# A fused attention and gated MLP block on one core: a regrouped prologue, other engine lists, and full-array gate matmuls for the second to last chunk

## The chip, the cores and the metric

The kernel runs on one core of a Trainium2 chip. Its engines work side by side, each on its own list of instructions in the order written: PE (TensorE, matmuls, with PEld for its weight loads), ACT (ScalarE), DVE (VectorE), POOL (GpSimd) and SP (SyncE, which here only issues DMA transfers). They wait for each other through semaphores. The metric is the device time of one launch in microseconds, as the median of several runs. The kernel before takes 939.43 us (three runs, 938.72 to 939.80).

## The reference

Input x has 2048 rows of 640 values in bf16. A first half is attention without a mask, with 32 heads of 20 values each; a second half is a gated MLP of width 1728.

```python
h  = x + attention(layernorm(x), wqkv, 32 heads) @ wo
g  = layernorm(h) @ w_gate
u  = layernorm(h) @ w_up
h2 = h + (gelu(g) * u) @ w_down
```

Attention is softmax(q k^T / sqrt(20)) v for each head, so 32 x 2048 x 2048 exponentials are taken, about 134 million. The layer norms have no weights.

## The kernel before, in words

**A planner writes the order.** The kernel is not written as loops that run on the chip. Every operation is entered with its engine, an estimated duration, a priority, and the data it reads and writes (class Sched, method op). A list scheduler (method schedule) then picks, for each engine, what comes next by its own model of time, and emit writes one straight list of instructions for each engine with the waits that are needed. A change of a duration, a priority or an engine can so reorder everything behind it. Between two modes of an engine the planner adds a cost of its own, MODE_SWITCH, 0.1 for PE. PE has three modes in it: "row" (the score matmuls, 32 rows of the array each), "col" (32 columns of the array each) and "full" (the whole array). Where PE would be idle for long the planner inserts matmuls on dummy data, to keep the PE clock up (function idle; they read wo or x and gk).

**Prologue.** x is loaded by SP in eight transfers of two row tiles each (a row tile is 128 rows; list XLS gives the tiles of each transfer). The q and k part of wqkv is loaded when the transfer that holds tile 4 has landed, the v part when the one with tile 11 has landed (XG), and wo after that. For each group of four tiles come the statistics of the layer norm (ln_stats on DVE, or ln_stats_act on ACT, by list LNS), 1/sqrt(variance) for the four together (ln_rsqrt: sqrt on ACT, reciprocal on DVE), the normalisation itself (ln_apply, by list LNE), five PE transposes, and the copy of their result from PSUM (list LNV). Statistics of a tile on ACT are two passes with a read of the accumulator behind each. Then proj makes k of the first four heads for all 2048 rows and q for the first 512, with priorities G0P; proj_v makes v. The first score matmul needs all of these.

**Attention.** Queries go in seven chunks, of 512, 512, 256, 256, 256, 128 and 128 rows (CHUNKS). The chunks are cut in 32 slots, and each slot in 64 score tiles of 128 x 512, 2048 tiles in all. A unit is two or three tiles: PE makes their scores (row mode) in two or three PSUM banks, ACT takes the exponential of all banks of the unit in one instruction, PE multiplies by v (col mode) into bank 6. List PATS says for each slot whether units alternate between three and two tiles ('2') or are all of three tiles ('3'). List DS says, for each slot as a hex digit, how many units give their third tile to DVE, which computes the exponential in integer and polynomial steps (d_exp), two tiles together.

**MLP and what lies behind a chunk.** When the slots of a chunk are done, function post enters its output projection, second layer norm (here ln_rsqrt has no sqrt, but a bit trick and two Newton steps on DVE), transposes, gates, ups and downs. They run as background work of PE and DVE under the attention of the next chunks. Gate results are copied by DVE (L1081) into an SBUF array, ACT applies gelu to it later in a few long instructions (each time it has to change its function table), DVE multiplies by the ups (L1100), and the downs are added to h by DVE (L1117). For chunk 5, the second to last (GT = (5,)), gelu, ups and downs are held until the last exponential, but its gates run under the attention of chunk 6. In background work a 128-column matmul is issued as four matmuls of 32 columns of the array each (quarters, line 664 of the profile). Operations carry an alternative as one full-array matmul (whole, line 660) that the planner uses only before the first and after the last score matmul.

The tail is what follows the last exponential: the rest of chunk 5, and all that chunk 6 needs.

Of the kernel before, what the change touches and what calls it, by code (L numbers as in the profile page):

```python
# [6 lines left out]
ALU = mybir.AluOpType  # L7
# [3 lines left out]
I32 = mybir.dt.int32  # L11
# [7 lines left out]
DMA_RATE = 0.36  # L19
DT = 0  # L20
LATE = (0, 1, 2, 3, 4)
LNS = [{'a': 'act', 'd': 'dve'}[x] for x in 'dddddaaaddddddaa']
LNE = [{'a': 'act', 'd': 'dve', 'p': 'pool'}[x] for x in 'dddadaddddaaadda']
LNV = [{'a': 'act', 'd': 'dve'}[x] for x in 'dadadddaadaaadad']
SLIP = 0.0
WARM = 3.4
KEEP = 0.5
# [23 lines left out]
class Sched:  # L51
# [10 lines left out]
    def op(self, eng, fns, dur, prio, reads=(), writes=(), acq=(), rel=(), after=(), sem=None, lat=None, mode=None, mb=0.0, alt=None):  # L62
        if self.evp is not None and eng == "dve" and rel and prio >= P_EPI:
            prio = self.evp
        o = Op()
        o.i = len(self.ops)
        o.eng, o.dur, o.lat, o.sem = eng, dur, LAT[eng] if lat is None else lat, sem
        o.mode = mode
        o.mb = mb
        o.alt = alt  # L70
        o.tag = writes[0] if writes else None
        o.fns = fns if isinstance(fns, list) else [fns]
        o.prio = (prio, o.i)
        deps = set(after)
        for r in reads:
            if r in self.lw:
                deps.add(self.lw[r])
        for w in writes:
            if w in self.lw:
                deps.add(self.lw[w])  # L80
            deps.update(self.rd.get(w, ()))
        for r in reads:
            self.rd.setdefault(r, []).append(o.i)
        for w in writes:
            self.lw[w] = o.i
            self.rd[w] = []
        deps.discard(o.i)
        o.deps = deps
        o.acq = list(acq)
        o.rel = list(rel)  # L90
        o.succ = []
        o.ready = 0.0
        o.start = None
        o.group = None
        self.ops.append(o)
        return o.i
# [230 lines left out]
RSQRT_MAGIC = float(0x5F3759DF)  # L327
# [12 lines left out]
VAG = 13  # L340
P1E = 'dd'
P1 = 1
XLS = (2,2,2,2,2,2,2,2)
XG = (4,11)
POOLT = 1.0
LNM = 'd'
# [6 lines left out]
XLAG = 0.85  # L353
XLG0 = 0.5
HG = 1
GT = (5,)
XPL = 1
KPR = 3.0
TFIRST = 0.0
PRE = 0.2  # L360
G0P = (2.5, 1.5, 2.5, 2.5, 1.5)
G0E = [{'a': 'act', 'd': 'dve'}[x] for x in 'dddda']


def bass_sequential_preLN__mha_block__glu_gated_geglu__prompt_kernel(
# [12 lines left out]
    with ExitStack() as es:  # L378
        sc = Sched(nc)
        op = sc.op  # L380
# [4 lines left out]
        def I(method, *args, **kwargs):  # L385
            return lambda eng: getattr(eng, method)(*args, **kwargs)  # L386


        def c_mm(n, passes=1):
            return 0.003 + passes * n / 2400.0  # L390
# [92 lines left out]
        def bank(b, n=512):  # L483
            return PS[:, 512 * b.b:512 * b.b + n]
# [45 lines left out]
        def xkey(t):  # L530
            return xof[t]

        xof, t0 = [], 0
        for i, n in enumerate(XLS):
            xof += [f"x_{i}"] * n
# [40 lines left out]
        def ln_rsqrt(t0, n, prio, need_nm=0):  # L576
            ts = range(t0, t0 + n)
            y, v = rs[:, t0:t0 + n], mv[:, t0:t0 + n, 1]
            a, b = nw[:, 0, 0:n], nw[:, 1, 0:n]
            vk, rk = [("mv", t) for t in ts], [("rs", t) for t in ts]  # L580
            d = lambda fn, r, w: op("dve", fn, 0.14, prio, reads=r, writes=w)
            if need_nm:

                op("act", I("activation", a, v, ACT.Sqrt, bias=epsc[:, 0:1]), 0.19, prio, mode="sqrt", reads=vk + ["eps"], writes=["nw0", "sd"])
                d(I("reciprocal", y, a), ["nw0"], rk)
                if need_nm == 1:
                    d(I("scalar_tensor_tensor", out=nm[:, t0:t0 + n], in0=y, scalar=-1.0, in1=mv[:, t0:t0 + n, 0],
                        op0=ALU.mult, op1=ALU.mult), rk + vk, [("nm", t) for t in ts])
                return
            d(I("tensor_scalar", a, v, LN_EPS, None, ALU.add), vk, ["nw0"])  # L590
            d(I("tensor_scalar", b.bitcast(I32), a.bitcast(I32), 1, None, ALU.logical_shift_right), ["nw0"], ["nw1"])
            d(I("tensor_scalar", y.bitcast(I32), b.bitcast(I32), -1.0, RSQRT_MAGIC, ALU.mult, ALU.add), ["nw1"], rk)
            for _ in range(2):
                d(I("tensor_tensor", b, y, y, ALU.mult), rk, ["nw1"])
                d(I("scalar_tensor_tensor", out=b, in0=b, scalar=-0.5, in1=a, op0=ALU.mult, op1=ALU.mult),
                  ["nw0", "nw1"], ["nw1"])
                d(I("scalar_tensor_tensor", out=y, in0=b, scalar=1.5, in1=y, op0=ALU.add, op1=ALU.mult),
                  ["nw1"] + rk, rk)

        def ln_apply(eng, src, dst, dkey, t, rkeys, prio):  # L600
# [32 lines left out]
        def sc_id():  # L633
            _id[0] += 1
            return _id[0]
# [4 lines left out]
        for t0 in range(0, NT, 4):  # L640
            sa = [t for t in range(t0, t0 + 4) if LNS[t] == "act"]
            for t in range(t0, t0 + 4):
                (ln_stats_act if t in sa else ln_stats)(x_sb[:, t, :], t, [xkey(t)], P_EPI)
            if sa:
                assert sa == list(range(sa[0], sa[-1] + 1))
                op("dve", I("tensor_scalar", mv[:, sa[0]:sa[-1] + 1, 1], mv[:, sa[0]:sa[-1] + 1, 1], 1.0 / D, None, ALU.mult), 0.14,
                   P_QK, reads=[("mv1", t) for t in sa], writes=[("mv", t) for t in sa])
            ln_rsqrt(t0, 4, P_QK, 1)
            for t in range(t0, t0 + 4):
                e_ops.append(ln_apply(LNE[t], x_sb[:, t, :], xn_p[:, t % 4, :], ("xnp", t % 4), t, [xkey(t)], P_QK))  # L650
                transposes(xn_p[:, t % 4, :], [("xnp", t % 4)], xnT[:, :, t * 128:(t + 1) * 128], ("xnT", t),
                           ALLB, P_EPI, LNV[t])
                e_ops.append(len(sc.ops) - 2)
# [5 lines left out]
        def whole(out, l, r, start, stop):  # L659
            return [lambda eng: eng.matmul(out()[0:l.shape[-1]], l, r, start=start, stop=stop, skip_group_check=True)]  # L660

        def quarters(out, l, r, start, stop):
            m = l.shape[-1]
            return [lambda eng, j=j: eng.matmul(out()[j:j + 32], l[:, j:j + 32], r, start=start, stop=stop,  # L664
                                                tile_position=(0, j), skip_group_check=True) for j in range(0, m, 32)]
# [97 lines left out]
            tiles += [(s_, g, kb, j) for g in gs for kb in range(NT // nk) for j in range(4)]  # L763
            slot_end.append(len(tiles))

        PATS = '22222222222322232222222332223322'
        DS = '06418768558877797888786986867867'
        PAT = [((0, 1, 2), (3, 4, 5)) if PATS[i] == '3' else ((0, 1, 2), (3, 4)) for i in range(len(slots))]
        units, ubank, upos = [], [], []
        i = 0  # L770
# [154 lines left out]
        for s_, (c, gs) in enumerate(slots):  # L925
            us = [u for u, tl in enumerate(units) if len(tl) == 3 and all(x[0] == s_ for x in tl)]
            n = int(DS[s_], 16)
            us = us[1:len(us) - DTAIL]
# [50 lines left out]
        def post(c, banks, tail):  # L979
            p = P_EPI if tail else P_BG - PRE * (c >= PREC)  # L980
            q0, nq = CHUNKS[c]
# [10 lines left out]
            for tt in range(nt):  # L992
# [10 lines left out]
                for hf in range(2):  # L1003
                    bk = Bank(*banks)
# [11 lines left out]
            if tail:  # L1016
                op("act", I("activation", nm[:, 0:1], off0[:], ACT.Gelu_apprx_tanh), 0.06, -1, mode="gelu", reads=["off0"],
                   writes=["pre"], after=(sc.lw["sd"],))
# [5 lines left out]
            p, pre = P_BG - TFIRST * tail, p  # L1024
# [11 lines left out]
            def mms(k, w, wkey, after, p=p):  # L1036
                bk, key = Bank(*banks), ("bk", sc_id())
                for fi in range(min(fn_, NF - k * fn_)):
                    f = k * fn_ + fi
                    mf = min(128, DFF - 128 * f)  # L1040
                    for a in range(NA):
                        st = fi == 0 and a == 0
                        op("pe", quarters(lambda fi=fi: bank(bk)[:, fi * nq:(fi + 1) * nq], w[:, a, f * 128:f * 128 + mf],
                                          hnT[:, a, hb * 128:hb * 128 + nq], a == 0, a == NA - 1),
                           c_mm(nq), p, mode="col", alt=whole(lambda fi=fi: bank(bk)[:, fi * nq:(fi + 1) * nq],
                                                              w[:, a, f * 128:f * 128 + mf], hnT[:, a, hb * 128:hb * 128 + nq],
                                                              a == 0, a == NA - 1), reads=hk + [wkey], writes=[key], acq=[bk] if st else [],
                           after=after if st else ())
                return bk, key
# [19 lines left out]
            else:  # L1069

                cp, gl = [], []
                for k in range(nb):
# [3 lines left out]
                    w_ = wid(k)  # L1076
                    if k >= nb - HG and c not in GT:
                        hold.append((k, bg, kg, m, fv, fk, w_))
# [3 lines left out]
                                 reads=[kg], writes=fk, rel=[bg], after=first))  # L1082
# [39 lines left out]

            if c in GT:
                def later(ba):
# [12 lines left out]
        if XPL:  # L1137
            op("act", I("activation", nm[:, 0:1], off0[:], ACT.Exp, scale=0.0), 0.06, P_QK, mode="exp", reads=["off0", ("xnT", 15), ("xnT", 14)],
               writes=["xpl", ("nm", 0)])
        for c in range(4):  # L1140
            proj("k", 0, c, PRO, G0P[c], G0E[c], True)
        proj("q", 0, 0, PRO, G0P[4], G0E[4], True)
        k3 = sc.lw["k", 0, 3]
# [16 lines left out]
        for s_, (c, gs) in enumerate(slots):  # L1160
            if c == 0:
                g = s_
# [70 lines left out]
```

## Time and profile before

| what | value |
|---|---|
| median of the runs | 939.43 us |
| the profiled execution | 939.73 us, span 937.9 us |
| ACT busy | 904.2 us, 96% of the span |
| PE busy | 877.7 us, 94% |
| DVE busy | 794.5 us, 85% |
| first exponential starts | 32.86 us |
| last exponential ends | 908.4 us |
| instructions | 33402 |
| granted TensorE clock | 1.0 over the span |

The span is the time from the first to the last instruction in the profiled execution; the 1.8 us between it and that execution's time lie outside the instructions. Nearly all lines of the program are entered through one helper, line 386, so groups are told apart by their tiles: exponentials write pts or rege from ps (PSUM), score matmuls read qt_all and kt_all, gates, ups and downs read regw (the weights). In a profile line a number behind x is a count of instructions. A time in square brackets is how long the engine sat idle before, and what ended that.

### The profile page before, as it was taken

Reading aid. Unit: us, or ns where it says so; the run is one execution under the profiler, and the core shown is the slowest. Engines: PE = TensorE matmul, PEld = TensorE weight load, DVE = VectorE, ACT = ScalarE, POOL = GpSimd, SP = SyncE. Lnnn points to the kernel's source line nnn. Section 1 sums busy time; section 2 is a strip of 40 time slices with the busy share of each in tenths; the row PEclk is TensorE's granted clock in tenths of the full one; section 3 lists DMA queues with packets and bytes.
Section 4 is the critical chain, followed back from the end, with each engine's and each line's share of the span. In section 5 each row is a group of like instructions: output and inputs, shape, how many; then the busy total and the mean of one; then the engine's idle time right before and its main releaser. Section 6 shows DMA issues by size and latency. Waiting matters only on the chain.

```text
span 937.9 us, 33402 instructions
## 1 busy us (share of the span) xinstructions
PE 877.7 (94%) x15201; PEld 386.6 (41%) x15203; DVE 794.5 (85%) x1749; ACT 904.2 (96%) x884; POOL 11.2 (1%) x45
## 2 busy tenths in 40 slices
PE   5999999999999989999999999999889999989998
PEld 3433332222233222323343333344445654556666
DVE  8659768999999999688999996988998787898673
ACT  7999999999999999999999999999999999999891
POOL 4000000000000000000000000000000000000000
PEclk9999999999999999999999999999999999999999
DMA  7010000000000160000100000011000010000000
GB/s 253 2 30 2 2 1 2 1 1 2 1 2 2 33 253 2 1 1 17 43 3 1 2 2 2 2 31 26 7 3 3 3 31 17 17 4 3 5 18 15
DMA packets 11820, 19.90 MB, mean 21 GB/s; under 512 B 608, under 2 KB 9760, under 8 KB 11680
## 3 DMA queue, kind: packets, MB, share of 16 engines
q1 hardware_dynamic: 11680, 17.78, 5.7%
q8 instruction: 119, 1.95, 0.9%
q14 instruction: 21, 0.17, 0.1%
HBM read 15.16 MB, written 2.62 MB: 19 GB/s over the span
## 4 chain that ended last, share of the span: by engine, by line
ACT 74%; PE 20%; DVE 4%; POOL 1%; issue 1%; POOLq 0%
ACT pts L386 44%; ACT rege L386 29%; PE ps L664 7%; PE ps L386 7%; PE ps L660 4%; DVE rege L386 2%; PE ps L618 1%; POOL regw L386 1%; DVE stats L386 0%; DVE qt_all L386 0%; PE ps L952 0%; DVE rege L1100 0%; DVE kt_all L694 0%; ACT L1087 0%; ACT rege L1087 0%
## 5 line engine op out<-in xcount | busy, mean ns | idle before, releaser
L386 ACT ACTIVATE pts<-ps 128x1024 bf16<-128x1024 f32 (+1 forms) x482 | 549.3, 1345 | 3.2 <-PE ps L386 3.0
L386 ACT ACTIVATE rege<-ps 128x1024 bf16<-128x1024 f32 (+1 forms) x312 | 363.6, 1328 | 1.4 <-PE ps L386 1.3
L386 PE MATMUL ps<-qt_all,kt_all 32*128 32x256 bf16 (+2 forms) x3584 | 311.2, 288 | 36.1 <-ACT pts L386 16.4
L386 PEld LDWEIGHTS ps<-qt_all,kt_all 32*128 32x128 bf16 x3584 | 96.5, 92 | 275.8 <-ACT pts L386 130.6
L664 PE MATMUL ps<-rege,regw 128*32 128x256 bf16 (+2 forms) x2970 | 158.7, 308 | 5.1 <-issue 2.3
L386 PE MATMUL ps<-pts,v_all 128*21 128x256 bf16 (+2 forms) x1956 | 157.7, 292 | 0.4 <-DVE osb L386 0.3
L386 PE MATMUL ps<-rege,v_all 128*21 128x256 bf16 (+2 forms) x1394 | 129.4, 294 | 0.0
L664 PE MATMUL ps<-regw 128*32 128x512 bf16 (+1 forms) x1656 | 120.5, 358 | 1.0 <-DVE v_all L749 0.5
L386 DVE TENSOR_TENSOR rege<-rege 128x1024 bf16<-128x1024 bf16 (+3 forms) x170 | 108.4, 641 | 1.0
L386 DVE TENSOR_SCALAR qt_all<-ps 128x512 int16<-128x512 f32 x110 | 75.3, 685 | 16.0 <-PE ps L386 15.5
L664 PEld LDWEIGHTS ps<-rege,regw 128*32 128x32 bf16 x2970 | 73.3, 96 | 37.6 <-issue 17.5
L386 DVE TENSOR_SCALAR rege<-rege 128x1024 bf16<-128x1024 int16 (+3 forms) x225 | 87.3, 398 | 1.3
L386 DVE TENSOR_TENSOR qt_all<-qt_all 128x1024 bf16<-128x1024 bf16 (+3 forms) x124 | 82.3, 664 | 1.2
L664 PE MATMUL ps<-regw,rege 128*32 128x320 bf16 x1484 | 79.3, 301 | 0.3 <-DVE rege L1100 0.3
L386 DVE TENSOR_SCALAR rege<-ps 128x512 int16<-128x512 f32 x103 | 70.5, 684 | 9.0 <-PE ps L386 8.5
L386 DVE TENSOR_SCALAR qt_all<-qt_all 128x1024 bf16<-128x1024 int16 (+3 forms) x182 | 73.3, 408 | 1.9
L386 PEld LDWEIGHTS ps<-pts,v_all 128*21 128x21 bf16 x1956 | 46.4, 90 | 60.6 <-issue 52.5
L386 PEld LDWEIGHTS ps<-rege,v_all 128*21 128x21 bf16 x1394 | 38.4, 90 | 42.1 <-issue 35.1
L386 PE MATMUL ps<-wo,gk 128*21 128x256 bf16 x296 | 52.6, 274 | 0.0
L664 PEld LDWEIGHTS ps<-regw 128*32 128x32 bf16 x1656 | 37.8, 95 | 34.8 <-issue 15.9
L1100 DVE TENSOR_TENSOR rege<-rege,ps 128x512 bf16<-128x512 bf16 (+2 forms) x53 | 35.8, 676 | 13.1 <-PE ps L664 12.8
L664 PEld LDWEIGHTS ps<-regw,rege 128*32 128x32 bf16 x1484 | 35.8, 95 | 22.2 <-issue 13.7
(109 smaller groups left out, 727.3 us busy)
## 6 DMA issues: line engine op xcount, KB each, us to landing
rege<-in_A_x_dram SPq DMA_DIRECT2D x11, 320.0 KB, 4.7
out_dram<-rege SPq DMA_DIRECT2D x16, 160.0 KB, 1.9
regw<-in_B_w_gate_dram SPq DMA_DIRECT2D x1, 2160.0 KB, 9.2
regw<-in_B_w_up_dram SPq DMA_DIRECT2D x1, 2160.0 KB, 14.1
regw<-in_B_w_down_dram SPq DMA_DIRECT2D x1, 2080.0 KB, 19.2
rege<-in_A_wqkv_dram SPq DMA_DIRECT2D x1, 1600.0 KB, 9.0
rege<-in_A_x_dram SPq DMA_DIRECT2D x2, 640.0 KB, 4.4
regw<-in_A_wqkv_dram SPq DMA_DIRECT2D x1, 800.0 KB, 8.0
```

The costliest lines, as they stand in the source:

```text
L386: return lambda eng: getattr(eng, method)(*args, **kwargs)
L618: op("pe", lambda eng, a=a: eng.transpose(bank16(bk, D)[:, 128 * a:128 * a + 128], src[:, a * 128:(a + 1) * 128], ident[:]), 0.056, prio, ...
L660: return [lambda eng: eng.matmul(out()[0:l.shape[-1]], l, r, start=start, stop=stop, skip_group_check=True)]
L664: return [lambda eng, j=j: eng.matmul(out()[j:j + 32], l[:, j:j + 32], r, start=start, stop=stop, tile_position=(0, j), skip_group_check=T ...
L1100: hdone.append(op("dve", lambda eng, bu=bu, fv=fv, m=m, w_=w_: eng.tensor_tensor(fv, fv, bank(bu, w_)[0:m, :], ALU.mult), c_dve(w_), p, re ...
```

## The change

- XLS goes from eight transfers of two tiles to five of 2, 2, 4, 4 and 4 tiles. By XG the q and k weights then wait for a transfer of tiles 4 to 7, in the place of 4 and 5; the v weights wait for tiles 8 to 11, in the place of 10 and 11.
- LNS, LNE, LNV: other tiles go to ACT. Statistics on ACT for 4 tiles in the place of 5, normalisation on ACT for 9 in the place of 6, copies on ACT for 7 in the place of 8.
- G0P: other priorities for the first projections.
- The bit trick in ln_rsqrt takes one DVE instruction less (the shift is folded into a multiplication by -0.5). The path with LNG is not used, as LNG is 0.
- PATS has seven slots with '3' in the place of six, and DS sums to 216 tiles in the place of 213; both also move between slots.
- The gates of chunk 5 are full-array matmuls (FW = 1): 70 matmuls in the place of 270, entered in mode "full".

```diff
-LNS = [{'a': 'act', 'd': 'dve'}[x] for x in 'dddddaaaddddddaa']
-LNE = [{'a': 'act', 'd': 'dve', 'p': 'pool'}[x] for x in 'dddadaddddaaadda']
-LNV = [{'a': 'act', 'd': 'dve'}[x] for x in 'dadadddaadaaadad']
+LNS = [{'a': 'act', 'd': 'dve'}[x] for x in 'dddaddaaddddddda']
+LNE = [{'a': 'act', 'd': 'dve', 'p': 'pool'}[x] for x in 'daaadaaaadadaddd']
+LNV = [{'a': 'act', 'd': 'dve'}[x] for x in 'dddaadddadaaddaa']
...
-XLS = (2,2,2,2,2,2,2,2)
+XLS = (2, 2, 4, 4, 4)
...
+LNG = 0
+LNGT = 0.2
+FW = 1
...
-G0P = (2.5, 1.5, 2.5, 2.5, 1.5)
+G0P = (2.2, 1.5, 0.5, 2.2, 0.5)
...
-            d(I("tensor_scalar", b.bitcast(I32), a.bitcast(I32), 1, None, ALU.logical_shift_right), ["nw0"], ["nw1"])
-            d(I("tensor_scalar", y.bitcast(I32), b.bitcast(I32), -1.0, RSQRT_MAGIC, ALU.mult, ALU.add), ["nw1"], rk)
+            d(I("tensor_scalar", y.bitcast(I32), a.bitcast(I32), -0.5, RSQRT_MAGIC, ALU.mult, ALU.add), ["nw0"], rk)
...
-        PATS = '22222222222322232222222332223322'
-        DS = '06418768558877797888786986867867'
+        PATS = '22222222222332232222223332223222'
+        DS = '03518768559878787888887976887868'
...
-                        op("pe", quarters(lambda fi=fi: bank(bk)[:, fi * nq:(fi + 1) * nq], w[:, a, f * 128:f * 128 + mf],
+                        wh = FW and c in GT
+                        op("pe", (whole if wh else quarters)(lambda fi=fi: bank(bk)[:, fi * nq:(fi + 1) * nq], w[:, a, f * 128:f * 128 + mf],
                                           hnT[:, a, hb * 128:hb * 128 + nq], a == 0, a == NA - 1),
-                           c_mm(nq), p, mode="col", alt=whole(lambda fi=fi: bank(bk)[:, fi * nq:(fi + 1) * nq],
+                           c_mm(nq), p, mode="full" if wh else "col", alt=None if wh else whole(lambda fi=fi: bank(bk)[:, fi * nq:(fi + 1) * nq],
```

More of the change, by code (lines that the diff above doesn't have):

```diff
@@ L590, in ln_rsqrt @@
             d(I("tensor_scalar", a, v, LN_EPS, None, ALU.add), vk, ["nw0"])
-            d(I("tensor_scalar", b.bitcast(I32), a.bitcast(I32), 1, None, ALU.logical_shift_right), ["nw0"], ["nw1"])
-            d(I("tensor_scalar", y.bitcast(I32), b.bitcast(I32), -1.0, RSQRT_MAGIC, ALU.mult, ALU.add), ["nw1"], rk)
-            for _ in range(2):
-                d(I("tensor_tensor", b, y, y, ALU.mult), rk, ["nw1"])
-                d(I("scalar_tensor_tensor", out=b, in0=b, scalar=-0.5, in1=a, op0=ALU.mult, op1=ALU.mult),
+            d(I("tensor_scalar", y.bitcast(I32), a.bitcast(I32), -0.5, RSQRT_MAGIC, ALU.mult, ALU.add), ["nw0"], rk)
+            if LNG:
+                g = lambda fn, r, w: op("pool", fn, LNGT, prio, reads=r, writes=w)
+            else:
+                g = d
+            for _ in range(2):
+                g(I("tensor_tensor", b, y, y, ALU.mult), rk, ["nw1"])
+                if LNG:
+                    g(I("tensor_tensor", b, b, a, ALU.mult), ["nw0", "nw1"], ["nw1"])
+                    g(I("tensor_scalar", b, b, -0.5, 1.5, ALU.mult, ALU.add), ["nw1"], ["nw1"])
+                    g(I("tensor_tensor", y, y, b, ALU.mult), ["nw1"] + rk, rk)
+                    continue
+                g(I("scalar_tensor_tensor", out=b, in0=b, scalar=-0.5, in1=a, op0=ALU.mult, op1=ALU.mult),
                   ["nw0", "nw1"], ["nw1"])
-                d(I("scalar_tensor_tensor", out=y, in0=b, scalar=1.5, in1=y, op0=ALU.add, op1=ALU.mult),
+                g(I("scalar_tensor_tensor", out=y, in0=b, scalar=1.5, in1=y, op0=ALU.add, op1=ALU.mult),
                   ["nw1"] + rk, rk)
```

## The prediction, made before the changed kernel was run

> **What bounds the kernel now.** I read the page first, then a table of stages, then the waits of the late stage and its timeline.
>
> ```profile
> span 937.9 us, 33402 instructions
> PE 877.7 (94%) x15201; PEld 386.6 (41%) x15203; DVE 794.5 (85%) x1749; ACT 904.2 (96%) x884; POOL 11.2 (1%) x45
> q8 instruction: 119, 1.95, 0.9%
> ```
>
> ACT is busy 96% of the span. PE with its weight loads is 30,404 of the 33,402 instructions, and they are fetched by a queue of their own: 119 packets, so about 256 instructions in each (30,404 / 119 = 255.5). The table of stages shows where each engine is full.
>
> ```profile
> core 0: us, PE busy (x) PEld busy (x) DVE busy (x) ACT busy (x) POOL busy (x), PEclk, DMA share, GB/s
> 4.00:10.00 6.00, 0.00 (x0) 0.00 (x0) 5.84 (x21) 3.08 (x8) 5.05 (x17) 1.00 1.02 347
> 16.50:26.00 9.50, 9.31 (x96) 6.42 (x99) 9.10 (x28) 9.31 (x17) 0.41 (x1) 1.00 0.32 91
> 32.90:842.00 809.10, 767.86 (x12627) 310.09 (x12630) 701.61 (x1526) 807.02 (x764) 0.00 (x0) 1.00 0.05 16
> 877.50:886.30 8.80, 6.47 (x297) 4.72 (x286) 2.75 (x6) 6.20 (x7) 0.00 (x0) 1.00 0.02 4
> 886.30:908.40 22.10, 21.77 (x669) 13.49 (x670) 20.31 (x44) 22.08 (x23) 0.00 (x0) 1.00 0.04 12
> 908.40:938.00 29.60, 25.87 (x330) 20.26 (x328) 11.33 (x25) 8.90 (x12) 0.00 (x0) 1.00 0.05 18
> ```
>
> From 32.9 to 842 us ACT is idle for 2.1 of 809 us: the exponentials set the time. In the tail (908.4 on) PE is the busiest. One stretch, 877.5 to 886.3, has all three engines idle at once: PE for 2.3 us, ACT for 2.6, DVE for 6. Its rows, from the waits of PE and the timelines of ACT and PE:
>
> ```profile
> PE ps L664 <- issue: 2.3, 3, 1.1
> ```
> ```profile
> 882.65 1.45 ACT L386 ACTIVATE pts<-ps 128x1536 bf16<-128x1536 f32 x1 [1.22 <-PE ps L386]
> ...
> 886.29 1.94 ACT L386 ACTIVATE rege<-ps 128x1024 bf16<-128x1024 f32 x2 [1.27 <-PE ps L386]
> ```
> ```profile
> 878.19 0.51 PE L664 MATMUL ps<-rege,regw 128*32 128x128 bf16 x17 [0.30 <-issue]
> ...
> 881.93 0.34 PE L664 MATMUL ps<-rege,regw 128*32 128x128 bf16 x9 [0.87 <-issue]
> ...
> 885.68 0.23 PE L664 MATMUL ps<-rege,regw 128*32 128x128 bf16 x1 [1.13 <-issue]
> ```
> ```profile
> 881.90:885.65 3.75, 2.62 (x128) 1.00 0.02 4
> ```
>
> PE stops three times, 0.30 + 0.87 + 1.13 = 2.3 us, and waits for no other engine. Each stop stands before a gate matmul of chunk 5 (128-wide, line 664), in the middle of a run of them. The restarts are 3.74 and 3.75 us apart, and between two of them there are 128 matmuls, with as many weight loads 256 instructions: one packet. So PE has eaten its stock of instructions and gets 256 in each 3.75 us, 14.6 ns for each. ACT's two waits, 1.22 + 1.27 = 2.49 us, end right behind the second and third stop, on score matmuls queued behind the gates. The Trainium skill, "Runtime: NRT & Kernel Launch", section "Instruction fetch mechanics", says that instructions come in blocks of 256 and that crossing a block is mostly hidden. The trace agrees with the 256; in this stretch it isn't hidden (0.30, 0.87, 1.13 us).
>
> **The change part by part.**
>
> *Gates of chunk 5 as full-array matmuls.* 270 matmuls become 70, and with their weight loads 400 instructions less. At 14.6 ns each that is 5.8 us less to fetch, more than the 2.3 us lacking. So I take all three stops away. Against it stand streaming and mode changes; rows from the chain of waits and from PE's timeline:
>
> ```profile
> 853.60 0.39 PE ps L618 x5
> ```
> ```profile
> 876.84 0.22 PE ps L664 x16
> ```
> ```profile
> 922.60 8.33 PE L660 MATMUL ps<-rege,regw 128*128 128x128 bf16 x140
> ```
>
> Quarters run at 0.22 / 16 = 13.8 ns while instructions last, 270 of them 3.7 us. Full ones run at 8.33 / 140 = 59.5 ns (here in the tail), 70 of them 4.2 us: +0.5 us. Five full-array transposes between two other modes cost 0.39 us where five at 59.5 would cost 0.30: 0.09 us for the change of mode. The gates lie in about 11 bursts; some half of them follow a score matmul directly, where a mode change is paid today too, the others follow v matmuls of the same mode and would pay one more: +0.5 us (0 to 1.0). In PE's account: -2.3 + 0.5 + 0.5 = -1.3 us; in ACT's: -2.5 us, if the planner puts the bursts where ACT doesn't wait. PE is nearly full from 886 us to the end, so what PE pays comes out in the tail. I take the middle, **-1.8 us**. Bounds: -2.5, and +1.5 if the stops stay (0.5 + 1.0). The Trainium skill, "TensorEngine Tiling (Array Packing)", section "Key Properties", speaks against the change: changing the tiling mode drains the array. The 0.09 us agrees with it; were it paid by every burst at both ends (22 x 0.09 = 2.0), PE's account would be +0.2 and the part worth nothing.
>
> *PATS and DS.* The price of an exponential, from the chain:
>
> ```profile
> 94.46 4.09 ACT pts L386 x4
> 98.55 2.75 ACT rege L386 x3
> ```
>
> Three of two tiles take 2.75 us, 0.917 each; four with one of three tiles 4.09, so that one 1.34. A tile costs 0.423 us, an instruction by itself 0.07. Cutting the 2048 tiles by the two lists gives 794 exponentials before and 790 after, on 1835 and 1832 tiles: 3 x 0.423 + 4 x 0.07 = 1.55 us less on ACT. ACT is never idle for long between 33 and 842 us, so this comes out nearly whole; what falls in the last two slots, where PE is full, may not. I take **-1.3 us** (0 to -1.55). DVE pays for it:
>
> ```profile
> L386 DVE TENSOR_TENSOR rege<-rege 128x1024 bf16<-128x1024 bf16 x112 | 76.4, 684 | 0.8
> L386 DVE TENSOR_SCALAR qt_all<-ps 128x512 int16<-128x512 f32 x110 | 75.3, 685 | 16.0 <-PE ps L386 15.5
> L386 DVE TENSOR_SCALAR rege<-rege 128x1024 bf16<-128x1024 int16 x112 | 46.8, 419 | 1.0
> ```
> ```profile
> 240.00:360.00 120.00, 114.70 (x251) 1.00 0.16 57
> ```
>
> Two tiles take 2 x 0.685 + 3 x 0.684 + 4 x 0.419 = 5.1 us, so three more tiles up to 7.7 us. DVE is idle for 143 us of the span, but for only 5.3 between 240 and 360 us, where slot 10 gets one tile more and where nothing stands between DVE being full and ACT waiting for banks. I cost it at nothing, with that cover; a rival below takes it away.
>
> *The shorter bit trick.* One DVE instruction of a chain of eight less, for six chunks, all under attention (this is chunk 5's, on the path neither before nor after; ACT's exponentials hide it):
>
> ```profile
> 868.64 0.15 DVE L386 TENSOR_SCALAR nw<-nw 128x1 int32<-128x1 int32 x1
> ```
>
> 6 x 0.15 = 0.9 us of DVE, taken as 0.
>
> *Prologue.* SP's issues, ACT's first work, the wait for the weights, and the prices:
>
> ```profile
> 0.75 4.49 SPq L386 DMA_DIRECT2D rege<-in_A_x_dram  x8
> 6.47 0.37 SPq L386 DMA_DIRECT2D rege<-in_A_wqkv_dram  x1
> ```
> ```profile
> 6.47 0.74 ACT L386 ACTIVATE xn_t<-rege 128x640 bf16<-128x640 bf16 x1 [4.24 <-DMA rege<-in_A_x_dram]
> ```
> ```profile
> POOL regw L386 <- DMA rege<-in_A_wqkv_dram: 2.7, 1, 2.7
> ```
> ```profile
> L386 DVE BATCH_NORM_STATS2 stats<-rege 128x6 f32<-128x320 bf16 x22 | 9.5, 465 | 0.4 <-DMA rege<-in_A_x_dram 0.3
> L386 DVE TENSOR_SCALAR rege<-rege,mv,rs 128x640 bf16<-128x640 bf16 x10 | 4.1, 458 | 0.0
> L628 DVE COPY regw<-ps 128x640 bf16<-128x640 bf16 x8 | 3.8, 478 | 0.3 <-PE ps L618 0.2
> ```
> ```profile
> L386 ACT ACTIVATE rege<-rege,nm,rs 128x640 bf16<-128x640 bf16 x6 | 5.3, 915 | 0.2 <-DVE nm L386 0.2
> L625 ACT ACTIVATE regw<-ps 128x640 bf16<-128x640 bf16 x8 | 5.3, 702 | 0.2 <-PE ps L618 0.2
> L386 ACT ACTIVATE xn_t<-rege,mv 128x640 bf16<-128x640 bf16 x5 | 4.1, 815 | 0.0
> ```
>
> Work: ACT does 3 normalisations more (+2.7 us), one set of statistics less (two passes, -1.6) and one copy less (-0.7): +0.4. DVE does statistics of one tile more (+0.9), 3 normalisations less (-1.4), one copy more (+0.5): 0. Start: ACT sits idle for 4.24 us, until tile 5 lands at 6.47. Now its first tile is number 3, of the second transfer. That has the same size as before and two transfers, each some 0.9 us (0.33 MB at the 347 GB/s of the row from 4 to 10 us), less ahead of it than tile 5's, so ACT starts some 1.6 us earlier, and the rsqrt of the first four tiles no longer queues behind a long tile on ACT. Earlier start less added work, shared by two engines that are both full from 16.5 to 26 us: (1.6 - 0.4) / 2 = 0.6; with fewer DMA issues on SP (4.49 / 8 = 0.56 us each, three less, not on the path but in favour) I take **-0.7 us**. Against it: the q and k weights are issued when the four-tile transfer lands, which is two tiles or about 0.9 us later than 6.47. They stand behind the rest of x in the queues anyway, so most of this is hidden; if not, POOL's pad waits 0.9 us longer and all projections behind it. Order by G0P can gain or lose as much again. Bounds: -2.0 and +2.0.
>
> **Sum.** -1.8 - 1.3 - 0.7 = -3.8 us. The profiled execution took 939.73 us, 1.8 more than its span and 0.3 more than the median; taken from the median, 939.43 - 3.8 = **935.6 us**.
>
> **The rivals.**
>
> 1. *The gates give nothing.* The stops go, but mode changes and slower streaming spend it on a PE that is full to the end, or the stops come from something else. For it: PE 98% busy from 886 us. Against: the 128 matmuls between stops, and 0.09 us for a mode change. Late part 0: 939.4 - 2.0 = 937.4 us, and up to 938.9 at the bound of +1.5.
> 2. *The prologue gets longer.* The weights come 0.9 us later, and the PE, full from 16.5 us on, passes it all on; with a bad order +1.2 in the place of -0.7: 937.5 us.
> 3. *DVE becomes the bound, and the kernel slower.* The place is slots 8 to 13 (DVE idle 4%) and the last slot, which gets one tile more. If all 7.7 us fell where DVE is full, ACT would wait for it and its own saving be worth nothing: -1.8 - 0.7 + 7.7 = +5.2 us. It decides (over 0.2% slower) from 4.4 us, some 57% of the added work. At two thirds: 939.4 + 2.6 = 942.0 us. For it: the 95% between 240 and 360. Against: only one of the net additions lies there, and DVE idles 143 us in all.
>
> **How the numbers follow.** A measurement can tell about 0.2%, 1.9 us: faster is below 937.55, slower above 941.3. Forecast 0.62 (its own range 933.4 to 937.2, from -2.5 - 1.55 - 2.0 to the sum without the prologue's and half of the gates' gain); rival 1 0.14; rival 2 0.10; rival 3 0.14. Faster: 0.60 of the forecast, 0.05 of rival 2, 0.01 of rival 1 = 0.66. Slower: 0.13 of rival 3 and 0.01 of rival 2 = 0.14. Same: the remaining 0.20. The range goes from 932.9 (the sum of the best bounds, 933.4, and half a microsecond of scatter) to 940.2, which takes in rivals 1 and 2 and leaves out most of rival 3.
>
> **What would show it.** Right: no wait of PE on issue and no wait of ACT on PE over 1 us between 870 and 890; gates as 128*128 at about 60 ns; 790 exponentials; the first one some 0.7 us before 32.86, the last some 3 to 4 us before 908.4; a tail of about 29.5 us as now. Wrong: PE stops at other places, more L660 downs between the last exponential and the last layer norm (a longer tail), ACT waits in slots 8 to 13 while DVE is full, or the pad on POOL starting a microsecond later than now with the first exponential behind 33.

## The result, and the profile after

The changed kernel takes 935.92 us (median of 9 runs, 935.14 to 937.89), the kernel before 939.51 us over 9 runs. The ratio is 0.9963, with a 95% interval of 0.9955 to 0.9971: faster by 0.37%. Forecast were 935.6 us, in a range of 932.9 to 940.2.

The page of the changed kernel begins so; below it are its fetch queue and the table of stages (columns as before):

```profile
span 933.9 us, 32919 instructions
PE 877.2 (94%) x14957; PEld 385.5 (41%) x14959; DVE 797.4 (85%) x1762; ACT 902.6 (97%) x878; POOL 10.7 (1%) x45
q8 instruction: 117, 1.92, 0.8%
```
```profile
877.50:886.30 8.80, 8.80 (x231) 6.43 (x225) 5.71 (x12) 8.80 (x10) 0.00 (x0) 1.00 0.02 5
886.30:905.00 18.70, 18.34 (x513) 11.00 (x510) 17.38 (x36) 18.67 (x19) 0.00 (x0) 1.00 0.04 12
905.00:938.00 33.00, 25.90 (x306) 20.19 (x303) 11.05 (x24) 6.89 (x11) 0.00 (x0) 0.98 0.05 16
```

Between 877.5 and 886.3 PE and ACT were busy 6.47 and 6.20 of 8.80 us, and now both all the time (the last stretch of the table reaches 4 us past the end of the span). No wait of PE on issue is left between the first and the last exponential, and the gates are full-array matmuls that start some 57 ns apart (in the row below 1.07 us, less the 0.22 of one matmul, over 15):

```profile
877.58 1.07 PE L671 MATMUL ps<-rege,regw 128*128 128x128 bf16 x16
```

The fetch queue moved two packets less, and PE has 244 matmuls and as many weight loads less on record.

The span falls in three parts if it is cut at the first exponential and at the function table load behind the last one. Rows of ACT's timeline, before and then after:

```profile
32.86 3.71 ACT L386 ACTIVATE pts<-ps 128x1536 bf16<-128x1536 f32 x3
...
908.39 1.28 ACT L386 ACT_TABLE_LOAD   x1
```
```profile
33.38 3.71 ACT L389 ACTIVATE pts<-ps 128x1536 bf16<-128x1536 f32 x3
...
902.97 1.28 ACT L389 ACT_TABLE_LOAD   x1
```

| part | before, us | after, us | difference | forecast |
|---|---|---|---|---|
| prologue, to the first exponential | 32.86 | 33.38 | +0.5 | -0.7 |
| attention | 875.5 | 869.6 | -5.9 | -3.1, counting the middle value for the gates |
| tail, to the end of the span | 29.5 | 30.9 | +1.4 | 0 |
| span | 937.9 | 933.9 | -4.0 | -3.8 |

So the sum came out right and its parts did not. ACT's waits on PE in the attention part, before and then after:

```profile
ACT pts L386 <- PE ps L386: 3.0, 3, 1.6
ACT rege L386 <- PE ps L386: 1.3, 1, 1.3
```
```profile
ACT rege L389 <- PE ps L389: 0.4, 1, 0.4
```

4.3 us of waits became 0.4. The page counts 485 + 305 = 790 exponentials where there were 794; at the prices of the prediction that is 1.55 us less. 3.9 + 1.55 = 5.45 us of the 5.9. The rest is not waiting: ACT was busy 870.77 us of this part before and 868.65 after, 2.1 us less where the prices give 1.55. Of the 3.9 us, 2.49 are the two waits of the gates. Most of the others is one wait that the prediction had not looked at, since it read the waits one by one only for the late stage:

```profile
89.83 2.37 ACT L386 ACTIVATE pts<-ps 128x1024 bf16<-128x1024 f32 x2 [1.58 <-PE ps L386]
```

The tail grew, because more of the downs are left for it. Groups by form, PE, full-array downs, before and after:

```profile
L660 PE MATMUL ps<-regw,rege 128*128 128x320 bf16 x71 | 11.2, 300 | 0.5 <-DVE rege L1100 0.5
```
```profile
L671 PE MATMUL ps<-regw,rege 128*128 128x320 bf16 x83 | 13.0, 300 | 0.2 <-DVE rege L1112 0.2
```

Twelve more, at 320 columns and some 0.15 us each (1.8 us more busy), where PE is the busiest engine (27.9 us of a tail of 30.9): +1.4 us. The tail follows this count in the runs below too: 71 downs and 29.5 to 29.6 us, 74 and 29.7 to 30.1, 78 and 30.5, 83 and 30.9.

### The profile page after: what moved, and what is told of

Its sections match the earlier page's. It is cut to its first block, busy times and chain, and to the rows that moved or that the text cites. A ratio compares the mean times of both kernels' runs of the same rounds, so it can differ in the third digit from the quotient of the medians.

```text
span 933.9 us, 32919 instructions
## 1 busy us (share of the span) xinstructions
PE 877.2 (94%) x14957; PEld 385.5 (41%) x14959; DVE 797.4 (85%) x1762; ACT 902.6 (97%) x878; POOL 10.7 (1%) x45
## 4 chain that ended last, share of the span: by engine, by line
ACT 85%; PE 10%; DVE 2%; DMA 2%; issue 0%; SPq 0%; POOL 0%; POOLq 0%
ACT pts L389 51%; ACT rege L389 33%; PE ps L671 4%; PE ps L675 3%; PE ps L389 3%; DMA rege<-in_A_wqkv_dram 1%; DVE qt_all L389 1%; DMA rege<-in_A_x_dram 1%; DVE rege L389 0%; ACT L389 0%; ACT L1099 0%; PE ps L629 0%; DVE rege L1093 0%; ACT rege L1099 0%; DVE rege L1112 0%
## 5 line engine op out<-in xcount | busy, mean ns | idle before, releaser
L675 PE MATMUL ps<-rege,regw 128*32 128x256 bf16 (+1 forms) x2700 | 155.1, 317 | 3.3 <-DVE qt_all L744 0.8
L389 DVE TENSOR_TENSOR rege<-rege 128x1024 bf16<-128x1024 bf16 (+2 forms) x172 | 111.6, 652 | 0.9
L389 DVE TENSOR_SCALAR qt_all<-ps 128x512 int16<-128x512 f32 x112 | 76.8, 686 | 11.9 <-PE ps L389 11.5
L675 PEld LDWEIGHTS ps<-rege,regw 128*32 128x32 bf16 x2700 | 67.7, 96 | 37.5 <-issue 13.7
L389 DVE TENSOR_SCALAR qt_all<-qt_all 128x1024 int16<-128x1024 int16 (+3 forms) x187 | 74.0, 401 | 1.4
L675 PE MATMUL ps<-regw,rege 128*32 128x320 bf16 (+1 forms) x1432 | 70.8, 301 | 0.4 <-DVE rege L1129 0.3
L675 PEld LDWEIGHTS ps<-regw,rege 128*32 128x32 bf16 (+1 forms) x1432 | 34.6, 96 | 20.5 <-issue 10.1
```

## The experiments

### One part undone, or done alone

The first four ran on one chip beside the kernel before, which took 939.74 us in these runs.

**Gates as quarters again.**

```diff
-FW = 1
+FW = 0
```

> The changed kernel with the gates of chunk 5 as quarters again (FW = 0), all else as changed. Theory (PE runs out of instructions in the gates): three or so waits of PE on issue come back, 2 to 3 us together, 128 matmuls apart, with ACT waits on PE of about 2.5 us; the tail loses about 1 us of its 1.5 us of growth; time 937.0 (1 us slower than the changed kernel, 935.9). Rival (the gates' form is worth nothing; the gain came from the exponentials and a wait around 90 us): no waits on issue that ACT feels, 935.9 within 0.5.

Measured: 937.31 us (936.27 to 939.50), ratio to before 0.9976 [0.9966, 0.9985]. PE's timeline, and a window from restart to restart:

```profile
879.57 0.34 PE L389 MATMUL ps<-qt_all,kt_all 32*128 32x128 bf16 x8 [0.96 <-issue]
...
883.32 0.60 PE L963 MATMUL ps<-identf,osb 128*128 128x128 f32 x4 [1.12 <-issue]
```
```profile
879.57:883.32 3.75, 2.62 (x129) 1.00 0.02 4
```

Two stops came back, 2.1 us, and ACT waits of 0.91 and 1.02 us behind them. They stand before a score matmul and before a transpose, not before a gate, yet 3.75 us and 129 matmuls apart (one may lie over the edge of the window), just as before. So it isn't the gate matmul that stalls, but whichever instruction is next when a packet of 256 hasn't come.

**Full-array gates alone.** The kernel before with the last hunk of the change only:

```diff
-op("pe", quarters(...), c_mm(nq), p, mode="col", alt=whole(...), ...)
+wh = c in GT
+op("pe", (whole if wh else quarters)(...), c_mm(nq), p, mode="full" if wh else "col", alt=None if wh else whole(...), ...)
```

> The kernel before with nothing but full-array gates for chunk 5. Theory: no wait of PE on issue from 870 to 890 us and no ACT wait there; attention 2.5 us shorter, tail 1 to 1.5 us longer, as more downs are left over; time 938.2 (-1.3). Rival 1 (stops all gained, nothing given back): 937.0. Rival 2 (mode changes spend it): 939.5.

Measured: 937.05 us (936.55 to 937.47), ratio 0.9973 [0.9962, 0.9985]: -2.7 us, as rival 1 had it and twice what the theory gave. By the interval of the ratio it is 1.4 to 3.6 us; the profile (below) says 2.8. ACT's waits in the attention part are those without the gates' two:

```profile
ACT pts L386 <- PE ps L386: 1.8, 2, 1.6
```

Attention took 872.5 us (-3.0) and the tail 29.7 (+0.2), with 74 full-array downs where there were 71. The mode changes and the slower streaming that the prediction charged with 1.0 us are there on PE, but don't show in the end time. Counted in the traces by the shapes of the matmuls, PE changes its mode 46 times between 873 and 891 us where it did 32 times, and the start of a matmul behind a change comes some 0.09 us later than within a mode (0.15 us in the place of 0.05 to 0.06).

**The old prologue.** The changed kernel with the old XLS, LNS, LNE, LNV and G0P.

```diff
-XLS = (2, 2, 4, 4, 4)
-G0P = (2.2, 1.5, 0.5, 2.2, 0.5)
+XLS = (2,2,2,2,2,2,2,2)
+G0P = (2.5, 1.5, 2.5, 2.5, 1.5)
...
```

> The changed kernel with the old loads of x, the old engine lists and priorities of the prologue. Theory (the new prologue costs 0.5 us, since the q and k weights land 1.5 us later): first exponential back at 32.9 us in the place of 33.4, time 935.4. Rival (the new prologue gains behind the first exponential, in the v and k projections that it leaves over): 936.5 or more, with the first exponential at 32.9 and a longer attention part.

Measured: 935.38 us (935.09 to 936.37, 4 runs), ratio 0.9957 [0.9942, 0.9972]. The first exponential starts at 32.90, and attention takes 869.6 us as in the changed kernel. So the new prologue brings nothing that shows; whether it costs the 0.5 us is within the intervals. This run differs from the one before it by the lists of slots and the shorter bit trick alone, and is 1.7 us faster (935.38 against 937.05; the spans differ by 1.7 as well): attention 2.9 us shorter, the tail 1.2 longer. That is what the new lists bring on the old prologue.

**The old lists of slots.** The changed kernel with the old PATS and DS.

```diff
-        PATS = '22222222222332232222223332223222'
-        DS = '03518768559878787888887976887868'
+        PATS = '22222222222322232222222332223322'
+        DS = '06418768558877797888786986867867'
```

> The changed kernel with the old lists of slots (PATS and DS). Theory: ACT gets its 1.55 us of exponentials back, and the wait of ACT around 90 us (1.6 us, where DVE is full in the first slots) comes back: 939.0, about 3 us slower than the changed kernel. Rival (only the exponentials count, the wait at 90 us went away with the new prologue): 937.4.

Measured: 939.42 us (938.35 to 941.76), ratio 1.0000 [0.9991, 1.0010]: 3.5 us slower than the changed kernel, as the theory had it. The wait is back, at 90.62, in ACT's timeline and then its waits in the attention part:

```profile
90.62 2.37 ACT L389 ACTIVATE pts<-ps 128x1024 bf16<-128x1024 f32 x2 [1.56 <-PE ps L389]
```
```profile
ACT pts L389 <- PE ps L389: 2.1, 3, 1.6
ACT rege L389 <- PE ps L389: 0.8, 1, 0.8
```

Attention is 4.3 us longer (2.5 of waits more, 1.55 of exponentials), the tail 1.2 us shorter (29.8). But not all of the waits belong to the lists. 1.14 us of them stand at another place, which neither the kernel before nor the old lists on the old prologue (the run with full-array gates alone) show:

```profile
358.59 1.02 ACT L389 ACTIVATE pts<-ps 128x1024 bf16<-128x1024 f32 x1 [0.34 <-PE ps L389]
360.41 1.94 ACT L389 ACTIVATE rege<-ps 128x1024 bf16<-128x1024 f32 x2 [0.80 <-PE ps L389]
```

The run with full-array gates alone has the old lists too and takes 937.05 us, 2.4 less, with intervals that don't meet. So the new prologue (or the shorter bit trick, the only other difference) costs about 2.4 us on the old lists and hardly anything on the new ones. Why is not shown.

### What the stops in the gates come from

**Fewer instructions in front of the gates.** The kernel before, gates as they were, but the ups of chunk 4 full-array:

```diff
+wh = wkey == "wu" and c == 4
```

> The kernel before, its chunk-5 gates still 270 quarters, but the ups of chunk 4, which run just ahead of them (864 to 876 us, 256 columns wide), as 70 full-array matmuls in the place of 270: 400 instructions less in front of the gates. Theory (a stock of instructions that runs dry): 400 instructions are 5.8 us of fetching, the stops in the gates (2.3 us) go or shrink to under 0.5 us though the gates themselves are as before, and ACT's two waits with them; time about 937.2, as with full-array gates. Rival (the stops belong to the quarter gates themselves, their form or their weight loads): the three stops stay, 2 to 2.5 us, time 939.5 to 940.

Measured: 938.42 us (937.82 to 939.19), ratio 0.9991 [0.9981, 1.0000], beside a kernel before of 939.42. The expectation was half wrong. The stops shrink from 2.3 to 1.15 us and don't go:

```profile
883.07 0.23 PE L386 MATMUL ps<-rege,v_all 128*21 128x128 bf16 x2 [0.98 <-issue]
...
886.81 0.24 PE L664 MATMUL ps<-rege,regw 128*32 128x128 bf16 x3 [0.17 <-issue]
```
```profile
862.00:873.50 11.50, 11.05 (x201) 1.00 0.01 3
873.50:882.09 8.59, 8.58 (x344) 1.00 0.02 4
```

For 11.5 us PE ate only 402 instructions (201 matmuls and their weight loads), where 785 could have come at 14.6 ns each. Then it ate 688 in 8.59 us, where 586 could come, and stopped: by that rate some 100 had been in hand. So what is saved earlier isn't carried over.

The fetch queue shows why. In the traces its packets start one for about every 256 instructions that PE has eaten, however slowly it eats: in these 11.5 us only two, at 863.66 and 871.78, in the row of the queue:

```profile
q8 instruction: 2, 0.03, 1.1%
```

At all nine stops of four profiles (three in the kernel before, two each in this run, with quarters again and, below, with one digit of DS) it looks the same. The next packet starts 1.1 to 1.2 us after a restart, takes 0.9 to 1.3 us, and PE goes on 1.3 to 1.5 us after it has landed. So the 3.75 us look like the round trip of one packet that is fetched ahead, and PE stops where it eats 256 instructions clearly faster. What counts is how many instructions lie in the gates themselves.

**Half as many, but not full-array.** The kernel before with the gates as matmuls of 64 columns of the array.

```diff
+def halves(out, l, r, start, stop):
+    return [... tile_position=(0, j) ... for j in range(0, m, 64)]
...
+op("pe", (halves if wh else quarters)(...), c_mm(nq), p, mode="half" if wh else "col", ...)
```

> The kernel before with the gates of chunk 5 as matmuls of 64 columns of the array, two in the place of four, in a mode of their own for the planner: 140 matmuls in the place of 270, 260 instructions less, and still no full-array matmul. Theory (the count of instructions is what matters): no or under 0.3 us of waits on issue in the gates, no ACT wait over 0.5 us there, time 937.0 to 937.6, like the full-array gates. Rival (it takes the full array, or fewer instructions in front): stops of 1 us or more, 938.5 or more.

Measured: 937.20 us (936.77 to 937.91), ratio 0.9974 [0.9962, 0.9985], against 937.05 for full-array gates. (The gates are 135 matmuls here, as the last strip has only 64 columns. The ups of chunk 5 in the tail become halves too, and its tail is 30.1 us.) No stop is left, and of ACT's waits only those that were there without the gates:

```profile
880.29 1.03 PE L669 MATMUL ps<-rege,regw 128*64 128x128 bf16 x30
```
```profile
ACT pts L386 <- PE ps L386: 1.8, 2, 1.6
```

So full-array isn't what helps; fewer instructions for the same work is. The packets of the fetch queue agree with that, but no run changed the fetching itself.

### The wait at 90 us

**One digit of DS.** The kernel before, slot 1 with 3 tiles for DVE in the place of 6.

```diff
-        DS = '06418768558877797888786986867867'
+        DS = '03418768558877797888786986867867'
```

> The kernel before with one digit changed: slot 1 gives 3 tiles to DVE in the place of 6. Theory (DVE is full there, and ACT's wait of 1.6 us around 90 us comes of it): the wait goes, ACT has 3 x 0.42 = 1.3 us more of exponentials, time 939.4 (-0.3). Rival (the wait comes from PE or the order of the projections): the wait stays and the time rises by 1.3, to 941.0.

Measured: 939.35 us (938.97 to 942.44), ratio 1.0005 [0.9996, 1.0014], beside 939.42. The wait is gone. In the kernel before, PE had waited for DVE (for the copy of a v projection) as ACT's wait began:

```profile
88.30 0.59 PE L664 MATMUL ps<-regw 128*32 128x320 bf16 x12 [0.49 <-DVE v_all L749]
```

DVE between 60 and 90 us, in the kernel before and here:

```profile
60.00:90.00 30.00, 25.34 (x56) 1.00 0.09 24
```
```profile
60.00:90.00 30.00, 20.41 (x48) 1.00 0.08 24
```

Taking 5 us of DVE out of this stretch frees ACT of 1.6 us, and the three tiles cost ACT 1.3 us; attention is 0.75 us shorter in the profile (874.8), of which 0.4 are shorter waits in the gates, and the end time is the same. In the changed kernel the same digit is 3, and the tiles are given to DVE in later slots, where ACT doesn't have to wait for it.

### The five loads

**Weights issued earlier.** The changed kernel with the q and k weights behind the second load.

```diff
-XG = (4,11)
+XG = (3,7)
```

> The changed kernel, the q and k weights issued when the second transfer of x has landed (tiles 2 and 3) in the place of the third, the v weights when the third has landed in the place of the fourth. Theory (the prologue's end hangs on the q and k weights, which landed 1.5 us later): they land 1 us or more earlier, the first exponential starts at 32.4 to 32.9 in the place of 33.4, time 935.2. Rival (the weights then take bandwidth from x, and the last layer norms set the end): first exponential at 33.4 or later, time 935.9 or more.

Measured: 935.96 us (935.12 to 936.13), ratio 0.9962 [0.9949, 0.9975]. The weights are issued at 4.69 in the place of 8.35 and POOL's pad starts at 16.85, hardly earlier than the 17.10 of the changed kernel; first exponential at 33.53. The rival's numbers came out. An issue 3.7 us earlier brought a landing inside the scatter of the five-load profiles (15.22 to 17.39, below), so issue alone doesn't seem to be what they wait for; it is one profile.

**Eight loads with the new lists, six loads, and the changed kernel again.** The first of these ran twice, the second time beside the other two.

```diff
-XLS = (2, 2, 4, 4, 4)
+XLS = (2,2,2,2,2,2,2,2)
```

and `XLS = (2, 2, 2, 2, 4, 4)` for six.

> The changed kernel with x in eight loads again, the new engine lists and priorities kept. Theory (the loads bring the loss, the new lists a gain of some 0.5 us): the q and k weights land as before (pad on POOL at 15.6), first exponential at 32.4, time 935.0. Rival (the new lists only fit the five loads): first exponential at 33.4 or later, 935.9 or more.

> The changed kernel with x in eight loads and the new engine lists, once more with more rounds. Theory (five loads bring the q and k weights 1 us or more later, the new lists gain 0.5): 935.2, and 0.5 to 1.0 below the changed kernel, with the first exponential at 32.3 to 32.5. Rival (the difference of the earlier run was scatter of the prologue): both the same within 0.3.

> The changed kernel with x in loads of 2, 2, 2, 2, 4 and 4 tiles, so that the q and k weights wait for a transfer of two tiles (4 and 5) again. Theory (what delays the weights is that they are issued only when four tiles have landed): pad at 15.6, first exponential at 32.4, 935.2. Rival (a large load itself is what delays what comes behind it): pad at 16.3 or later, first exponential at 33 or later, 935.9.

> The changed kernel once more, beside the two that follow, on the same chip. 935.9 within 0.6; first exponential at 33.2 to 33.7, pad on POOL at 16 to 17.4.

| kernel | median, us | ratio to before | pad on POOL | first exponential |
|---|---|---|---|---|
| changed, again | 936.12 (934.67 to 936.63) | 0.9958 [0.9945, 0.9970] | 15.22 | 32.28 |
| eight loads | 935.20 (934.49 to 935.92) | 0.9957 [0.9943, 0.9972] | 15.54 | 32.34 |
| eight loads, again | 935.20 (934.97 to 936.47) | 0.9954 [0.9942, 0.9967] | 14.76 | 32.88 |
| six loads | 936.02 (935.74 to 936.70) | 0.9960 [0.9946, 0.9973] | 15.55 | 33.19 |

The changed kernel, profiled a second time, has its weights almost 2 us earlier than the first time; the two rows of POOL, first and second profile:

```profile
17.10 1.10 POOL L389 COPY regw<-rege 128x400 bf16<-128x400 bf16 x2 [4.46 <-DMA rege<-in_A_wqkv_dram]
```
```profile
15.22 1.27 POOL L389 COPY regw<-rege 128x400 bf16<-128x400 bf16 x2 [2.56 <-DMA rege<-in_A_wqkv_dram]
```

So the landing of the weights scatters by as much as the whole effect, and one profile can't settle it. The repeat missed the expected ranges of pad and exponential, though not of the time. Nor does the landing alone set the first exponential: with eight loads the earlier pad (14.76) came with the later exponential (32.88), and six loads had the early pad of their theory, but neither its exponential nor its time. Over all profiles taken here: five loads, by the change's own XG, 17.10, 16.12, 17.39 and 15.22; eight loads 15.64, 14.84, 15.69, 16.46, 15.61, 15.54, 14.76 and 16.32. Means 16.5 and 15.6. That speaks for five loads being the later ones, but not safely, and what delays them stays open. The eight-load version with the new lists has the lowest median both times, 0.7 and 0.9 us under the changed kernel, within the intervals. It is no settled gain.

## Why the prediction was right, and where its steps were not

**The gates: mechanism right, size too small.** The step "PE has eaten its stock of instructions" holds: stops 3.74 or 3.75 us apart in four profiles, 128 or 129 matmuls where they were counted, on whatever matmul comes next, gone with half or a quarter of the matmuls. The term was -1.8 us, between an account for PE (-1.3) and one for ACT (-2.5). Alone, the full-array gates measured -2.7 us. What failed is the step from PE's account to the time, "what PE pays comes out in the tail". PE did pay, with 14 mode changes more and an estimated 14 x 0.09 = 1.3 us, more than the 0.5 charged; yet the tail took 0.2 us, and ACT's account (-2.5) is the one that came out. The price of 14.6 ns for each instruction saved ("5.8 us less to fetch") holds only where PE stops; the same 400 saved a little earlier (full-array ups) removed half of the stops.

**The slots: size wrong, by a wait not looked at.** The term was -1.3 us for the exponentials, in a stretch where ACT "is never idle for long". It has one wait of 1.58 us at 89.83, and DS takes three tiles from just there. The lists, with the shorter bit trick, brought 1.7 us on the old prologue: 1.55 of exponentials and 1.4 of waits (that one is gone, one of 0.4 us at 765 is new), less 1.2 of a longer tail. So the term came out near its size by two items that it left out. Undoing them in the changed kernel costs 3.5 us, with the 1.14 us of waits at 358 to 361 that neither the kernel before nor the changed one has. Rival 3, DVE becoming the bound, didn't come: nothing was paid at slot 10, nor at slot 13, which also gets one more and which the prediction left out ("only one of the net additions lies there").

**The prologue: wrong.** The term of -0.7 us came of ACT starting earlier, and it does: its first tile starts at 5.05 in the place of 6.47. But the end of the prologue didn't follow, at 33.4 in the first profile and 32.3 in the second, and with the old prologue the median is 0.5 us lower. Of the sum's steps, "they stand behind the rest of x in the queues anyway" did not hold in the first profile: the weights came 1.5 us later. In the second they came 0.4 us earlier than before and the first exponential 0.6 us earlier, nearly as forecast, in an execution of 934.67 us; but the median of those five runs was 936.12. So the gain comes and goes with the first loads, and what moves them stays open. Rival 2 described it; its price of 1.2 us was more than what shows.

**The tail: without a term.** "A tail of about 29.5 us as now" was wrong by +1.4 us. The prediction had named more downs there as a sign of being wrong, but its sum had no term for them. When ACT's part shrinks by 5.9 us and PE's background work under it stays the same, part of that work is pushed behind the last exponential: 12 more full-array downs.

The parts add up if they are taken one after the other: full-array gates 939.74 to 937.05, then the new lists and the shorter bit trick (which no run took alone) to 935.38, then the new prologue to 935.92 (this last one from other runs). That is -2.7, -1.7 and +0.5 us, where the prediction had -1.8, -1.3 and -0.7. Undone singly in the changed kernel they are worth +1.4 for the gates (937.31), +3.5 for the slots (939.42) and about -0.5 for the prologue; the parts depend on each other, though for the gates (1.4 against 2.7) the intervals still meet.

So the way and the cause of the largest term were right, but that 935.6 was met so closely is luck: gates and slots were priced 1.3 us too low together, and a prologue that was off by 1.2 us, in sign too, offset it. By stages it is the same: attention 2.8 us better than forecast, the tail 1.4 and the prologue 1.2 worse.

## What to carry to other kernels

When an engine stands idle on issue and waits for nobody, count the instructions between two stops: equal counts at equal distances point to the stream of instructions as the limit, and the packets of the fetch queue can confirm it. Then doing the same work in fewer instructions, at that very place, is worth more than its own busy time says. Read the waits of the engine that sets the time over the whole span, not only where the change is, since one wait of 1.6 us was worth as much as all exponentials saved. And when the bounding engine is relieved, ask what the others did under its cover: here a quarter of the gain came back as a longer tail.

## What the runs showed of the hardware

PE got its instructions at no more than 256 in 3.75 us, 14.6 ns each, where it stopped; four-way split matmuls of 128 columns run at 13.8 ns each, with a weight load each, 6.9 ns for an instruction, twice as fast as they were brought there. The packets come one at a time, one for about every 256 instructions eaten (119 packets for 30,404), and the 3.75 us split like a round trip: 1.1 to 1.2 us from a restart to the start of a packet, 0.9 to 1.3 us of transfer, 1.3 to 1.5 us from its landing to the next restart. A change between row, column and full mode of PE puts some 0.09 us between two matmuls (0.15 us from start to start in the place of 0.05 to 0.06). The attention part repeats to a hundredth: 869.59 us in the first and the second profile of the changed kernel (902.97 - 33.38, 901.87 - 32.28). The landing of the first loads does not, with 1.9 us between the same two profiles.
